# Decay rows read from SBUF, a warming of three matmuls, weight loads behind the rows, and a scheduler that counts transfers at 262 KB per microsecond

## The chip, the cores and the metric

The kernel runs on one core of one Trainium2 chip. The metric is device microseconds of one execution; a lower number is better. The core has five engines with their own queues, each of which works strictly in the order of its program: TensorE (PE, matmuls; its weight loads appear as PEld), VectorE (DVE), ScalarE (ACT), GpSimd (POOL) and SyncE (SP, which here issues the transfers). Engines wait for one another through semaphores. SBUF is the on-chip memory, PSUM holds matmul results in eight banks, HBM is the memory outside.

## The reference

Two parts are computed one behind the other: causal attention with a cumulative decay for 64 heads (8 batches of 8 heads, 576 positions, head size 64), and a feed-forward layer with softplus on the 4608 resulting rows.

```python
scores = scale * np.matmul(q, k.transpose(0, 1, 3, 2))
cum = np.cumsum(np.log(np.clip(f, 0.0001, 1.0)), axis=-1)
decay = cum[:, :, :, None] - cum[:, :, None, :]
scores = np.where(causal, -1000000000.0, scores + decay)
attn = softmax(scores)
x = np.matmul(attn, v)              # then (4608, 512)
h = x @ w_in                        # 512 -> 2048
g = np.maximum(h, 0.0) + np.log1p(np.exp(-np.abs(h)))
out = g @ w_out                     # 2048 -> 512
```

## The kernel before

**Jobs.** Attention is cut into jobs. Jobs 0 to 3 take two heads each of batch 0 and their first 256 positions; jobs 4 to 11 take one head each of batch 0 and its other positions; then follow 56 whole heads of batches 1 to 7. The first twelve are "plain": q, k and two extra rows lie as full fp32 in one of two tiles (T00 and T01, each with two places), and one fp32 matmul per piece makes the scores. The two extra rows hold the cumulative decay of the queries and of the keys and a constant 8 against it, so that the matmul itself adds the decay. Later jobs use tiles T0 and T1, in which q, k and the decay are split into a high and a low part; `raw` is the one buffer into which their q and k are loaded.

**Decay.** `decay` (L358) loads f for all 64 heads, clips it on VectorE (L366), takes the logarithm on ScalarE (L369) and sums along the positions with one scan on VectorE (L374) into the tile `cum`. The sums are stored to HBM (`cum_d`, L377), and the rows of the plain jobs are loaded from there (L639 for a pair of jobs, L644 and L645 for the others). `split` (L382, L383) makes the high and low parts `chl`, which are stored to HBM too (`aug_d`, L387), for the later jobs.

**A job.** `scores` (L747 where plain) fills a PSUM bank of the tag `att`; VectorE takes the row minimum (L754, tile `negm`), ScalarE the exponential (L774), VectorE the inverse sums (L786, L787); the weights are scaled (L796 and L798), turned by matmuls with an identity (L831, tile `b`), copied to SBUF, multiplied with v (L880 where plain, tile `o`), and the result is copied to `x` (`x32`).

**Feed-forward.** Tokens are taken in blocks; block 0 (256 tokens) is plain fp32: `h` (L1024) is the up-projection, in two PSUM banks that take turns; ScalarE makes |h|, exp and log (L1076 to L1082), VectorE adds them to `g` (L1088), and `acc` (L1147) is the down-projection. Later blocks use split numbers (L1043, L1128).

**Weights.** w_in and w_out come as 64-bit floats in 32 tiles of 512 KB, into five staging places (tags `wl` twice, `xh` twice, `xl` once; names `sti`, `sto`, `xh_st`, `xl_st`; L432). Each is converted by a scaling on ScalarE (L436), a clip on VectorE or GpSimd (L439), and three instructions on VectorE (L443, L447, L451; results `woh`, `wol`). A staging place is free again after L447.

**The scheduler.** `Plan.run` walks through all operations at build time, with a cost for each, and writes them to the engines in the order in which it expects them to start; the hardware then follows that order. SP is one of the engines that it plans: a transfer costs SP `on_dma` and lands `dma_lag` later. Where it expects TensorE to idle over 0.5 us before the first down-projection, it writes matmuls without a use there (`fill`, L1320), and `warm` (L1309) writes `WARM` such matmuls at the start. `decay_rest` and the loads of v and of weights are added to the plan at fixed points of `tile_decay_attention_softplus_ffn`.

Of the kernel before, what the change touches and what calls it, by code (L numbers as in the profile page):

```python
# [10 lines left out]
F32 = mybir.dt.float32  # L11
# [3 lines left out]
ALU = mybir.AluOpType  # L15
# [7 lines left out]
COPY_BIAS = 0.1  # L23
WINDOW = 700
PLAIN = 0
WARM = 7
FFN_RANK = 0
# [185 lines left out]
def tile_decay_attention_softplus_ffn(  # L213
# [21 lines left out]
    P = 128  # L235
# [41 lines left out]
    T = {}  # L277
# [22 lines left out]
    aug_d = dpool.tile([BH, 2, S], F32, name="aug_d")  # L300
    cum_d = dpool.tile([BH, S], F32, name="cum_d")

# [52 lines left out]

    decay_ready, cum_used, first_rows = {}, [], []

    def decay():  # L358
        box = {}

        def load(e):
            box["f"] = buf("wl", [P, 1024], "fs")[0:BH, 0:S]
            e.dma_start(out=box["f"], in_=f)

        def clip(e):
            e.tensor_scalar(box["f"], box["f"], 1e-4, 1.0, ALU.max, ALU.min)  # L366

        def log(e):
            e.activation(box["f"], box["f"], AF.Ln)  # L369

        def scan(e):

            box["c"] = buf("x32", [P, NCC, S], "cum")[0:BH, 0, :]
            e.tensor_tensor_scan(box["c"], box["f"], box["f"], 0.0, ALU.add, ALU.min)  # L374

        def store_first(e):
            e.dma_start(out=cum_d, in_=box["c"])  # L377

        def split(e):
            hl = buf("raw", [P, 2, S], "chl", F32R)  # L380
            ch, cl = box["hl"] = hl[0:BH, 0, :], hl[0:BH, 1, :]
            e.tensor_copy(ch, box["c"])  # L382
            e.tensor_sub(cl, box["c"], ch.bitcast(F32))  # L383
# [8 lines left out]
        c = add(On("DVE", 1.36), scan, after=[l], takes=("x32",))  # L392
        give("wl", [c])
        decay_ready["sums"] = add_dma(store_first, BH * S / 256, after=[c])
        cum_used.append(add(NO_ENGINE, mark, after=[decay_ready["sums"]]))
# [180 lines left out]
    def attention(job):  # L576
# [28 lines left out]
        def load_v():  # L605
# [12 lines left out]
            if plain:  # L618
                vtag = st["vtag"] = ("vhl", "vhl", "vraw", "vhl", "vraw")[number % 5]
            st["v"] = add_dma(v, 128 if pair else 160, takes=(vtag,))  # L620
            st["V"] = [st["v"]]

        def load32():
            def qk(e):
# [5 lines left out]
                else:  # L630
                    e.dma_start(out=qk32[0:64], in_=qkT[b, :, heads[0]])

            def rows(e):
                if pair:

                    t0 = T0[number // 2 % 2].rearrange("p t s -> p (t s)")[:, 0:2048]
                    t0 = t0.rearrange("p (i t s) -> p i t s", i=4, t=2)
                    for x in range(2):
                        e.dma_start(  # L639
                            out=t0[64 + x : 65 + x, :, x],  # L640
                            in_=cum_d[bh : bh + 4, 0:256].unsqueeze(0),
                        )
                else:
                    e.dma_start(out=qk32[64:65, 0, qs:qe], in_=cum_d[bh : bh + 1, qs:qe])  # L644
                    e.dma_start(out=qk32[65:66, 1, 0:ke], in_=cum_d[bh : bh + 1, 0:ke])  # L645

# [5 lines left out]
            if not pair:  # L652
                y = add_dma(rows, 4, 2, after=[start, decay_ready["sums"]] + set_)
# [6 lines left out]
            st["T"] = [x, y]  # L660

# [65 lines left out]
        def stat_tile(ti):  # L727
# [42 lines left out]
            for a, z, acc, box in todo:  # L770
# [4 lines left out]

                x = add(on_act(z - a, 0.19, True), weight, after=mins + [st["p"]] + ps_set)
                give("att", [x])
# [517 lines left out]
    for i in range(1, 4):  # L1295
        set_rows0(i)
    ps_set = [fill(x, 0.0, w, [decay_ready["sums"]]) for xs in ps for x, w in zip(xs, PW)]
# [26 lines left out]
    for n in range(len(jobs) + 1):  # L1324
# [87 lines left out]
```

## Time and profile before

| | us |
|---|---|
| median of three runs (1227.13 to 1228.07) | 1227.53 |
| the profiled execution | 1227.12 |
| its span | 1225.1 |
| start of the first scores | 14.30 |
| start of the first up-projection | 67.29 |
| start of the first down-projection | 89.58 |

The profile's page gives the busy time of each engine over the span. A table by windows gives the same for chosen stretches: us of the stretch, then busy us and number of instructions for each engine, the TensorE clock that was granted as a share of full speed (PEclk), the share of time in which the transfer engines were busy, and GB/s. In the timeline each row has its start, its length and, in brackets, how long the engine had idled and for what. In the chain of waits each row has a start, a length and what ended the step before. The groups of one tile give the shortest, median and longest duration in ns. An fp32 matmul stands in the profile as two rows (x16 for 8 matmuls).

### The profile page before, as it was taken

Reading aid. Unit: us, or ns where it says so; the run is one execution under the profiler, and the core shown is the slowest. Engines: PE = TensorE matmul, PEld = TensorE weight load, DVE = VectorE, ACT = ScalarE, POOL = GpSimd, SP = SyncE. Lnnn points to the kernel's source line nnn. Section 1 sums busy time; section 2 is a strip of 40 time slices with the busy share of each in tenths; the row PEclk is TensorE's granted clock in tenths of the full one; section 3 lists DMA queues with packets and bytes.
Section 4 is the critical chain, followed back from the end, with each engine's and each line's share of the span. In section 5 each row is a group of like instructions: output and inputs, shape, how many; then the busy total and the mean of one; then the engine's idle time right before and its main releaser. Section 6 shows DMA issues by size and latency. Waiting matters only on the chain.

```text
span 1225.1 us, 19553 instructions
## 1 busy us (share of the span) xinstructions
PE 1199.9 (98%) x6320; PEld 993.9 (81%) x6320; DVE 869.5 (71%) x2164; ACT 872.9 (71%) x2120; POOL 137.4 (11%) x128
## 2 busy tenths in 40 slices
PE   7899999999999999999999999999999999999998
PEld 5666678888887888888888888888888888888886
DVE  6998889998787678877787778677866774223322
ACT  4676688878787788778886788788867873444543
POOL 3632012010001000110010100110010000000000
PEclk9999999999999999999999999999999999999999
DMA  7874435435446543744464446453565425211210
GB/s 199 254 207 143 137 91 153 111 90 166 128 141 179 166 133 117 228 145 128 137 197 136 141 130 197 139 168 104 153 186 155 138 80 172 69 52 52 86 52 35
DMA packets 100198, 168.38 MB, mean 137 GB/s; under 512 B 10496, under 2 KB 74008, under 8 KB 100096
## 3 DMA queue, kind: packets, MB, share of 16 engines
q1 hardware_dynamic: 100096, 167.13, 46.2%
q8 instruction: 50, 0.82, 0.3%
q14 instruction: 52, 0.43, 0.1%
HBM read 127.85 MB, written 39.24 MB: 136 GB/s over the span
## 4 chain that ended last, share of the span: by engine, by line
PE 84%; DVE 6%; DMA 4%; ACT 4%; issue 1%; SPq 1%; POOL 1%; DVEq 0%; POOLq 0%; ACTq 0%
PE h L1043 29%; PE acc L1128 28%; PE b L831 7%; PE o L886 6%; PE s L750 3%; PE s L749 3%; PE h L1024 2%; PE acc L1147 2%; PE o L880 2%; DMA raw<-in_qkT 2%; PE s L747 1%; ACT p L774 1%; DVE s L754 1%; DMA xh_st<-in_w_in 1%; DVE pl L846 1%
## 5 line engine op out<-in xcount | busy, mean ns | idle before, releaser
L1043 PE MATMUL h<-xh,wih 128*128 128x512 f32 (+1 forms) x576 | 229.5, 401 | 0.7 <-DVE pl L846 0.3
L774 ACT ACTIVATE p<-s,negm 128x288 f32<-128x288 f32 (+7 forms) x384 | 183.0, 479 | 50.3 <-DVE negm L754 46.6
L1043 PE MATMUL h<-xl,wih 128*128 128x512 f32 (+1 forms) x576 | 216.7, 379 | 0.0
L1090 DVE SCALAR_TENSOR_TENSOR h<-h,e 128x512 f32<-128x512 f32 x136 | 95.2, 700 | 136.0 <-ACT e L1082 135.9
L754 DVE CUSTOM_DVE_ANT_0 s<-s,cmask 128x288 f32<-128x288 f32 (+5 forms) x320 | 137.8, 436 | 72.1 <-PE s L750 61.6
L798 POOL TENSOR_SCALAR p<-p,rsum 128x448 f32<-128x448 f32 (+4 forms) x79 | 89.4, 1139 | 784.5 <-PE s L750 192.6
L1076 ACT ACTIVATE e<-h 128x512 f32<-128x512 f32 x144 | 85.7, 595 | 126.4 <-PE h L1043 124.5
L846 DVE TENSOR_TENSOR pl<-b,ph 128x64 fp32r<-128x64 f32 (+1 forms) x224 | 126.3, 569 | 35.0 <-ACT ph L209 33.1
L1043 PE MATMUL h<-xh,wl 128*128 128x512 f32 (+1 forms) x576 | 148.7, 380 | 0.0
L1128 PE MATMUL acc<-woh_dt_float32r,gh 128*128 128x512 f32 x352 | 143.1, 406 | 0.0
L1128 PE MATMUL acc<-woh_dt_float32r,gl 128*128 128x512 f32 x352 | 138.0, 392 | 0.0
L1128 PE MATMUL acc<-wol_dt_float32r,gh 128*128 128x512 f32 x352 | 137.3, 390 | 0.0
L831 PE MATMUL b<-ident,p 128*128 128x128 f32 x784 | 126.5, 274 | 4.8 <-POOL p L798 2.6
L1043 PEld LDWEIGHTS h<-xh,wih 128*128 128x128 f32 x576 | 108.8, 189 | 17.1 <-DVE gl L1098 0.8
L1043 PEld LDWEIGHTS h<-xh,wl 128*128 128x128 f32 x576 | 104.8, 188 | 21.7
L1043 PEld LDWEIGHTS h<-xl,wih 128*128 128x128 f32 x576 | 108.8, 189 | 14.6
L1098 DVE TENSOR_TENSOR gl<-h,gh 128x512 fp32r<-128x512 f32 x136 | 93.4, 687 | 35.1 <-ACT gh L209 34.1
L209 ACT CAST ph<-b 128x512 fp32r<-128x512 f32 (+1 forms) x171 | 85.3, 501 | 41.7 <-PE b L831 40.4
L831 PEld LDWEIGHTS b<-ident,p 128*128 128x128 f32 x784 | 94.4, 140 | 22.6 <-ACT p L796 3.5
L796 ACT ACTIVATE p<-p,rsum 128x192 f32<-128x192 f32 (+6 forms) x219 | 108.6, 556 | 3.4 <-DVE rsum L787 2.8
L749 PE MATMUL s<-T 128*64 128x64 f32 x336 | 98.2, 304 | 2.0 <-ACT p L774 1.3
L886 PE MATMUL o<-ph,vhl 128*128 128x448 f32 (+4 forms) x352 | 98.6, 294 | 0.0
(159 smaller groups left out, 2402.2 us busy)
## 6 DMA issues: line engine op xcount, KB each, us to landing
wl<-wil_d SPq DMA_DIRECT2D x72, 512.0 KB
raw<-in_qkT SPq DMA_DIRECT2D x112, 288.0 KB
g_d<-gh SPq DMA_DIRECT2D x96, 128.0 KB
g_d<-gl SPq DMA_DIRECT2D x96, 128.0 KB
vr<-in_vR SPq DMA_DIRECT2D x64, 160.0 KB
out<-ob SPq DMA_DIRECT2D x36, 256.0 KB
sto<-in_w_out SPq DMA_DIRECT2D x11, 512.0 KB
sti<-in_w_in SPq DMA_DIRECT2D x9, 512.0 KB
```

The lines of the kernel that those rows point to most:

```text
L749: e.matmul(o, qA[:, q0:end], kA[:, a:z], start=True, stop=False)
L754: e.tensor_tensor_reduce(out=box["o"], in0=box["o"], in1=cmask[0:n_q, right - w : right], scale=-0.125, scalar=m0 if i else 3.0e38, op0=AL ...
L774: e.activation(o, box["o"], AF.Exp, bias=m1, scale=-1.0, accum_out=acc)
L796: e.activation(a, a, AF.Copy, scale=f_)
L798: e.tensor_scalar(a, a, f_, None, ALU.mult)
L831: e.transpose(box["ps"][:, at : at + P], pt[pi][:, c : c + P], one)
L846: e.tensor_sub(box["l"], box["ps"][:, 0:w], box["h"].bitcast(F32))
L886: e.matmul(box["ps"][:, a - g0 : z - g0], st["vhl"][:, vc, :], pbox[x][:, o : o + z - a], start=i == 0 and m == 0, stop=i == len(todo) - 1 ...
L1043: e.matmul(o, l, r, start=m == 0, stop=m == 11)
L1090: e.scalar_tensor_tensor(h, h, 0.0, box["e"], ALU.max, ALU.add)
L1098: e.tensor_sub(box["l"], box["t"], box["h"].bitcast(F32))
L1128: e.matmul(st["acc", tt], l, r[fc], start=fc == 0 and m == 0, stop=fc == NFC - 1 and m == 2,)
```

## The change

The rows of the plain jobs are read from the SBUF tile `cum`; `cum_d` and its store are gone. The scan is cut in two (256 and 320 positions), and the rows of jobs 0 to 3 need the first part alone. The second pair's rows are issued from ScalarE's queue. `cum` is held until the last of the rows is read. `decay_rest` (split and store for later jobs) moves from the start to job 2. `WARM` goes from 7 to 3. Weight loads wait in the plan for the first scan instead of the first rows' landing; v of the last plain jobs waits likewise. An exponential waits for the clearing of its own p tile instead of all ten. SP's cost of a transfer is its size at 262 KB per us instead of 360.

```diff
+RATE = 262
-WARM = 7
+WARM = 3
 def on_dma(kb, n=1, eng="SP"):
-    return On(eng, max(0.6 * n, kb / 360 if eng == "SP" else 0.0))
+    return On(eng, max(0.6 * n, kb / RATE) if eng == "SP" else 1.5 * n)
 def dma_lag(kb, n=1, eng="SP"):
-    return 0.6 * (n - 1) + 2.1 + kb / n / 360 - on_dma(kb, n, eng).cost
+    each = 0.6 if eng == "SP" else 1.5
+    return each * (n - 1) + 2.1 + kb / n / RATE - on_dma(kb, n, eng).cost
...
         def scan(e):
-            box["c"] = buf("x32", [P, NCC, S], "cum")[0:BH, 0, :]
-            e.tensor_tensor_scan(box["c"], box["f"], box["f"], 0.0, ALU.add, ALU.min)
-        def store_first(e):
-            e.dma_start(out=cum_d, in_=box["c"])
+            c = cum[0] = buf("x32", [P, NCC, S], "cum")[0:BH, 0, :]
+            x = box["f"][:, 0:256]
+            e.tensor_tensor_scan(c[:, 0:256], x, x, 0.0, ALU.add, ALU.min)
+        def scan_rest(e):
+            c = cum[0]
+            x = box["f"][:, 256:S]
+            e.tensor_tensor_scan(c[:, 256:S], x, x, c[:, 255:256], ALU.add, ALU.min)
...
-        decay_ready["sums"] = add_dma(store_first, BH * S / 256, after=[c])
-        def rest():
-            s = add(On("DVE", 1.05, 0.0, True), split, after=[c], takes=("raw",))
+        def rest(after):
+            s = add(On("DVE", 1.05, 0.0, True), split, after=[c, *after], takes=("raw",))
...
+            later = first_rows if 3 < number < nplain else []
-            st["v"] = add_dma(v, 128 if pair else 160, takes=(vtag,))
+            st["v"] = add_dma(v, 128 if pair else 160, after=later, takes=(vtag,))
...
+            def rows2(e, x):
+                t0 = T0[number // 2 % 2].rearrange("p t s -> p (t s)")[:, 0:2048]
+                t0 = t0.rearrange("p (i t s) -> p i t s", i=4, t=2)
+                e.dma_start(out=t0[64 + x : 65 + x, :, x], in_=cum[0][bh : bh + 4, 0:256])
             def rows(e):
...
+                e.dma_start(out=qk32[64:65, 0, qs:qe], in_=cum[0][bh : bh + 1, qs:qe])
+                e.dma_start(out=qk32[65:66, 1, 0:ke], in_=cum[0][bh : bh + 1, 0:ke])
...
-                need = [start, decay_ready["sums"]] + set_ + T0_set[number % 4 + 1, 1]
-                y = rows_of[number] = add_dma(rows, 8, 2, after=need)
-                first_rows[:] = first_rows or [y]
+                need = [start, decay_ready["first"]] + set_ + T0_set[number % 4 + 1, 1]
+                y = rows_of[number] = [
+                    add_dma(lambda e, r=r: rows2(e, r), 4, eng="ACT" if number else "SP", after=need)
+                    for r in range(2)
+                ]
+                first_rows[:] = [decay_ready["first"]]
+            if not number % 2 or not pair:
+                cum_used.append(add(NO_ENGINE, mark, after=y))
...
-        if n == 1:
-            decay_rest()
+        if n == 2:
+            decay_rest(wrote[0][0][2:])
```

The order that the scheduler writes changes over the first 900 or so of TensorE's 5319 rows; behind them TensorE's rows are the same to the end. Three places, in the words of the order listings (buffer numbers at the ends of names; the first number behind a letter is the job or block):

SP at the start, before, from the load of v for job 4 on (`cum_d` is the copy in HBM, T00 and T01 hold jobs 0 to 3, `sti0` and `sti1` are the first two weight tiles):

```order
L615 DMA vr4_164<-in_vR 128x320
L377 DMA cum_d_105<-cum_162 64x576
L639 DMA T00_72<-cum_d_105 1x4x256 x2
L639 DMA T01_73<-cum_d_105 1x4x256 x2
L432 DMA sti0_186<-in_w_in 128x1024
L387 DMA aug_d_104<-chl_167 64x576 x2
L626 DMA T01_73<-in_qkT 64x4x256
L432 DMA sti1_233<-in_w_in 128x1024
```

SP at the same place in the change:

```order
L641 DMA T00_72<-cum_155 1x4x256 x2
L435 DMA sti0_167<-in_w_in 128x1024
L630 DMA T01_73<-in_qkT 64x4x256
L435 DMA sti1_202<-in_w_in 128x1024
L630 DMA T01_73<-in_qkT 64x4x256
L435 DMA xh_st_237<-in_w_in 128x1024 x2
```

The store of the sums, the rows of T01 and the store to `aug_d` no longer stand ahead of the weight tiles (the rows of T01 are on ScalarE's queue now, the store to `aug_d` stands behind nine weight tiles).

VectorE around the first `g`, which frees the first of the two `h` banks, before (20 tiles are converted ahead of these rows and one, `wol9`, ends with the first of them):

```order
L451 SCALAR_TENSOR_TENSOR wol9_dt_float32_727<-to8_693,wol9_dt_float32_727 128x512
L754 ISA s5_2_0_749,negm1_76<-s5_2_0_749,cmask_74 128x288
L754 ISA negm1_76 128x1
L754 ISA s5_2_288_753,negm1_76<-s5_2_288_753,cmask_74,negm1_76 128x288
L754 ISA negm1_76 128x1
L498 TENSOR_TENSOR wil0_765<-woh0_dt_float32_263,wih_101 128x512
L1088 SCALAR_TENSOR_TENSOR g0_0_771<-h0_0_679,e0_0_742 128x512
```

VectorE around the first `g` in the change:

```order
L804 TENSOR_SCALAR p0_512_94<-p0_512_94,rsum2_89 128x448
L454 SCALAR_TENSOR_TENSOR woh11_dt_float32_777<-ti11_766,woh11_dt_float32_777 128x512
L760 ISA s7_0_0_753,negm3_78<-s7_0_0_753,cmask_74 64x320
L760 ISA negm3_78 64x1
L446 TENSOR_SCALAR wol9_dt_float32_815<-to8_775 128x512
L760 ISA s7_1_0_761,negm3_78<-s7_1_0_761,cmask_74 128x448
L760 ISA negm3_78 128x1
L450 SCALAR_TENSOR_TENSOR wol9_dt_float32_815<-sto8_745,wol9_dt_float32_815 128x512
L1094 SCALAR_TENSOR_TENSOR g0_0_834<-h0_0_575,e0_0_783 128x512
```

`g` stands behind two more jobs' row minima (jobs 6 and 7) than before, and behind 20 whole conversions of weight tiles instead of 21.

TensorE ahead of the third up-projection `h0_2`, the first that needs a freed `h` bank, before:

```order
L831 MATMUL b5_2_842<-ident_66,p1_640_100 128x128
L1024 MATMUL h0_2_815<-x32_0_284,woh4_dt_float32_468 128x256
L1024 MATMUL h0_2_815<-x32_0_284,woh5_dt_float32_470 128x256
L1024 MATMUL h0_2_815<-x32_0_284,woh6_dt_float32_489 128x256
L1024 MATMUL h0_2_815<-x32_0_284,woh7_dt_float32_492 128x256
L747 MATMUL s6_2_0_862<-T01_73 128x288
```

TensorE at that place in the change:

```order
L837 MATMUL b6_1_823<-ident_66,p0_640_95 128x128 x2
L837 MATMUL b6_2_830<-ident_66,p0_384_93 128x128
L837 MATMUL b6_2_830<-ident_66,p0_512_94 128x128
L837 MATMUL b6_2_830<-ident_66,p0_640_95 128x128
L753 MATMUL s7_2_288_838<-T01_73 128x288
L1030 MATMUL h0_2_845<-x32_0_269,woh4_dt_float32_445 128x256
```

One more job is turned (job 6) and one more has its scores (job 7) ahead of `h0_2`; twelve fill matmuls (`fill`) stand ahead of the first of job 6's transposes.

More of the change, by code (lines that the diff above doesn't have):

```diff
@@ L352, in tile_decay_attention_softplus_ffn @@
     halves_set = []
-    decay_ready, cum_used, first_rows = {}, [], []
+    decay_ready, cum_used, first_rows, cum = {}, [], [], {}
     def decay():
@@ L391, in decay @@
         l = add(on_act(S), log, after=[o])
-        c = add(On("DVE", 1.36), scan, after=[l], takes=("x32",))
+        decay_ready["first"] = add(On("DVE", 0.63), scan, after=[l], takes=("x32",))
+        c = decay_ready["sums"] = add(On("DVE", 0.78), scan_rest, after=[decay_ready["first"]])
         give("wl", [c])
-        decay_ready["sums"] = add_dma(store_first, BH * S / 256, after=[c])
-        cum_used.append(add(NO_ENGINE, mark, after=[decay_ready["sums"]]))
-        def rest():
-            s = add(On("DVE", 1.05, 0.0, True), split, after=[c], takes=("raw",))
+        def rest(after):
+            s = add(On("DVE", 1.05, 0.0, True), split, after=[c, *after], takes=("raw",))
             w = add_dma(store, BH * S / 128, 2, after=[s] + first_rows)
@@ L652, in load32 @@
             if not pair:
-                y = add_dma(rows, 4, 2, after=[start, decay_ready["sums"]] + set_)
+                y = [add_dma(rows, 4, 2, after=[start, decay_ready["sums"]] + set_)]
             elif number % 2:
@@ L774, in weight @@
                     e.activation(o, box["o"], AF.Exp, bias=m1, scale=-1.0, accum_out=acc)
-                x = add(on_act(z - a, 0.19, True), weight, after=mins + [st["p"]] + ps_set)
+                x = add(on_act(z - a, 0.19, True), weight, after=mins + [st["p"], ps_set[number % 2, pi]])
                 give("att", [x])
@@ L1296, in tile_decay_attention_softplus_ffn @@
         set_rows0(i)
-    ps_set = [fill(x, 0.0, w, [decay_ready["sums"]]) for xs in ps for x, w in zip(xs, PW)]
+    ps_set = {
+        (j, i): fill(ps[j][i], 0.0, PW[i], [decay_ready["first"]])
+        for i in (3, 4, 2, 0, 1) for j in range(2)
+    }
     for n in range(nfirst):
```

18 lines of the change are left out of this document (3 added, 15 removed).

## The prediction

> **What bounds the kernel now.** I read the page's busy times first, for the whole span, then the windows, to find where TensorE's lost time lies.
>
> ```profile
> PE 1199.9 (98%) x6320; PEld 993.9 (81%) x6320; DVE 869.5 (71%) x2164; ACT 872.9 (71%) x2120; POOL 137.4 (11%) x128
> ```
>
> ```profile
> core 0: us, PE busy (x) PEld busy (x) DVE busy (x) ACT busy (x) POOL busy (x), PEclk, DMA share, GB/s
> 0.00:4.80 4.80, 2.45 (x11) 2.45 (x12) 2.70 (x14) 2.03 (x4) 4.01 (x18) 1.00 0.49 108
> 4.80:14.85 10.05, 10.05 (x47) 6.79 (x46) 4.49 (x9) 0.21 (x2) 1.60 (x4) 1.00 0.58 121
> 14.85:29.50 14.65, 10.82 (x67) 8.12 (x65) 11.71 (x44) 9.78 (x31) 2.61 (x5) 1.00 0.99 287
> 29.50:50.00 20.50, 16.24 (x102) 13.25 (x102) 18.09 (x36) 13.50 (x33) 13.95 (x10) 0.92 0.76 240
> 50.00:67.30 17.30, 15.62 (x101) 12.07 (x102) 17.02 (x42) 11.05 (x27) 10.86 (x5) 1.00 0.91 263
> ```
>
> TensorE is busy for 98% of the span, so anything to be gained is in its idle time and in matmuls without a use. Up to 67.3 us, where the first up-projection starts, it idles 2.35 + 3.83 + 4.26 + 1.68 = 12.1 us, and the fill matmuls hide more:
>
> ```profile
> sum 1225.10, PE 29.59 PEld 27.56; mean PE 5.92 PEld 5.51
> ```
>
> The start is one chain: f, clip, logarithm, scan, the store of the sums, their rows, the first scores. From 14.85 us the transfer engines are full (share 0.99), and from 50 us VectorE is (17.02 of 17.30). VectorE converts the weight tiles and makes the row minima, so **it decides when the first `g` is there** (L1088), and there the change must pay.
>
> **The start.** These are pieces of the chain of waits and of the timeline, the second fence for the weight loads of the warming.
>
> ```profile
> 4.77 1.36 DVE cum L374
> ...
> 6.14 3.66 DMA cum_d<-cum
> ```
>
> ```profile
> 6.56 0.34 PEld L1309 LDWEIGHTS warm<-cmask 128*128 128x128 f32 x1 [0.41 <-issue]
> 7.27 0.19 PEld L1309 LDWEIGHTS warm<-cmask 128*128 128x128 f32 x1 [0.37 <-issue]
> 7.64 0.19 PEld L1309 LDWEIGHTS warm<-cmask 128*128 128x128 f32 x1 [0.19 <-issue]
> ```
>
> ```profile
> 9.86 2.65 SPq L639 DMA_DIRECT2D T<-cum_d  x4
> ...
> 11.40 2.87 PEld L1320 LDWEIGHTS fill<-cmask 128*128 128x128 f32 x25 [0.19 <-issue]
> 12.55 0.44 SPq L432 DMA_DIRECT2D sti<-in_w_in  x1
> ...
> 14.30 3.50 PE L747 MATMUL s<-T 66*128 66x128 f32 x16
> ```
>
> Before, the scores start right behind the fill matmuls; the rows were issued by 12.5 us and did not hold them up visibly. In the change TensorE has 3 warming and 12 fill matmuls ahead of the scores, 6 and 24 halves. Warming halves are 0.71 us apart up to 7.27 us and 0.37 behind; the warming starts at 5.07, so three halves at 0.71 and three at 0.37 end near 8.4, and 24 fill halves at 2.87 / 25 = 0.115 take 2.75: **the first scores at 11.15, 3.1 us sooner.** The rows must be there by then. The first part of the scan is 256 of 576 positions, 1.36 x 256 / 576 = 0.60: done at 5.4. Two issues at 2.65 / 4 = 0.66 end at 6.75. No row shows a transfer from SBUF to SBUF; bounds are 0, and the 3.66 of the 144 KB store to HBM. The larger gives 10.4, still under 11.15, so I take the rows as covered by TensorE's queue; without that cover (shorter filling) they alone would let the scores start near 10. Pair two's issues lie on ScalarE's queue, 2 x 0.66 us that fall in its idle time (0.21 busy of 10.05). `cum` keeps its place longer; its next user in `x32` comes behind the last rows' issue, so I price that at nothing, and at one copy, 0.5 us, if it does wait.
>
> **The weight loads.** They leave SP at 6.75 instead of 12.55, 5.8 us sooner, because the store of the sums, whose landing the rows awaited, and two row issues are no longer ahead of them; `aug_d`, which stood between the first and the second tile, is behind them too. Were the transfer engines free then?
>
> ```profile
> 10.00:13.00 3.00, 3.00 (x20) 2.26 (x19) 0.00 (x0) 0.00 (x0) 0.00 (x0) 1.00 0.02 4
> 32.00:36.00 4.00, 3.00 (x14) 2.03 (x15) 4.00 (x6) 2.34 (x7) 3.91 (x4) 0.81 0.44 103
> 36.00:40.00 4.00, 4.00 (x29) 4.00 (x28) 3.96 (x11) 3.08 (x9) 1.26 (x1) 0.76 0.87 309
> ```
>
> At 10 to 13 us they moved 4 GB/s; the time is free, and what is loaded then is out of the way of the full stretch behind. Counting 262 KB per us is near what the full stretches move (263 and 287). The 240 of the window 29.5 to 50 is lower, so staging places, which come free by conversion, limit too.
>
> **VectorE up to the first `g`.** The third up-projection needs the `h` bank that this `g` frees.
>
> ```profile
> 0.00:77.37 77.37, 65.20 (x371) 50.00 (x372) 63.88 (x166) 45.68 (x115) 35.67 (x41) 0.98 0.79 224
> 67.30:89.65 22.35, 22.30 (x109) 16.16 (x107) 21.05 (x52) 18.78 (x45) 6.61 (x3) 1.00 0.69 192
> 89.65:175.00 85.35, 85.35 (x391) 56.00 (x392) 74.19 (x190) 60.10 (x151) 11.58 (x10) 1.00 0.45 130
> 175.00:280.00 105.00, 101.44 (x665) 88.37 (x664) 97.51 (x257) 85.75 (x227) 14.44 (x12) 1.00 0.42 118
> ```
>
> ```profile
> L451 DVE SCALAR_TENSOR_TENSOR woh_dt_float<-ti,woh_dt_float x16: 660/682/1095, 21.1 to 104.4; 128x512 uint32<-128x512 uint32 x16
> L439 DVE TENSOR_SCALAR ti<-ti x10: 416/424/755, 18.8 to 101.0; 128x512 f32<-128x512 f32 x10
> ```
>
> ```profile
> L754 DVE CUSTOM_DVE_ANT_0 s<-s,cmask x30: 274/432/633, 14.8 to 109.1; 128x128 f32<-128x128 f32 x8, 128x256 f32<-128x256 f32 x8, 64x320 f32<-64x320 f32 x5, 128x448 f32<-128x448 f32 x5
> ```
>
> 77.37 is the end of the first `g`; VectorE was busy 63.88 up to there and idle 13.5. In the new order it does more ahead of it: six more row minima, 288 to 448 wide, between the median 0.43 and the 0.63 of the widest plus a read of about 0.14, some 0.67 each: 4.0; three more clips that GpSimd did, at 0.42: 1.3; two more residual splits of the tile size of L451, at 0.68: 1.4; the rest (more sums, scalings and copies, the scan's second start, against one conversion less and a clearing that went to GpSimd) +0.4 by the nearest rows. Together +7.1: 71.0.
>
> Its idle time was 2.10 + 5.56 = 7.7 up to 14.85, and 5.8 behind. In the change the first 14.85 become 11.75 with 3.1 us less; of the work there, the split for `aug_d` (about 1.3) and one clearing (0.5) have moved behind, so 7.66 - 3.1 + 1.8 = 6.3 idle remain. The later 5.8 is waiting for tiles and clips, which come up to 5.8 us sooner and partly from VectorE itself: between 0 and 5.8 + 3.1 = 8.9 (the start's whole gain lost to later tiles). I take 4, nearer to the first because the loads gain more than the start. The first `g` ends at 71.0 + 6.3 + 4 = **81.3** (77.3 to 86.2). That is later than 77.37, yet TensorE has done more by then.
>
> **What TensorE has done by then.** The next rows give one matmul's price by the distances of starts.
>
> ```profile
> 82.64 1.03 PE L1024 MATMUL h<-x,woh_dt_float 128*128 128x256 f32 x4
> 83.50 0.92 PE L747 MATMUL s<-T 66*128 66x448 f32 x2
> 84.26 0.49 PE L831 MATMUL b<-ident,p 128*128 128x128 f32 x3
> 84.59 1.89 PE L1024 MATMUL h<-x,woh_dt_float 128*128 128x256 f32 x8
> 86.31 1.14 PE L747 MATMUL s<-T 66*128 66x288 f32 x4
> 87.38 2.27 PE L880 MATMUL o<-p,vr 128*64 128x320 f32 x10
> ```
>
> An up-projection matmul takes 0.86 / 2 = 0.43, a transpose 0.33 / 3 = 0.11, scores 0.76 at 448 wide and 1.07 / 2 = 0.535 at 288. Ahead of the new third up-projection stands, against what the old order had ahead of its first down-projection at 89.65: 12 more transposes (+1.3), four more score pieces (0.76, two of 0.535, one of 320 on 64 partitions at about 0.55: +2.4), and eight up-projections fewer (-3.5): +0.2. So at 81.3 it stands where the old one stood at 89.85, **8.5 us ahead** (3.6 to 12.5). TensorE itself can be there: from the first up-projection, which VectorE's share puts near 50 us, it has 20 us of work to the third.
>
> **What is kept.** At that point VectorE is behind: old, 63.88 - 10.07 (the overlap of both windows, 67.30 to 77.37, taken as full) + 21.05 = 74.9 us of work by 89.65; new, 71.0. The 4 us are still owed. VectorE idled 11.2 us from 89.65 to 175 and could pay there, but from 175 to 280 it is 93% busy; from about 280 us the two orders are the same. Kept is between 8.5 - 4.0 = 4.5 and 8.5; I take the middle, 6.5. The profiled execution of 1227.12 becomes 1220.6; the median shown stands 0.4 higher, so **1221.0**.
>
> **The rivals.**
> - *VectorE never waits behind 12 us.* If the earlier loads keep every tile ahead of it, `g` ends at 77.3, the gain is 12.5 and VectorE pays the rest later: 1215. Against: the full transfer engines above.
> - *The loads leave sooner and land no sooner.* If conversion, not issue, gates the staging places, VectorE's idle time stays, `g` is there at 86.2, the gain is 3.6 and the 4.0 of owed work eat it: about 1228, no change. For: the 240 GB/s between 29.5 and 50 with VectorE 18.09 of 20.50 busy.
> - *Slower: the loads into `raw`.* Later jobs load q and k into one buffer, and four such loads lie in the chain of waits between 180 and 300 us, the first and the last of them:
>
> ```profile
> 192.43 4.57 DMA raw<-in_qkT
> ...
> 267.59 4.45 DMA raw<-in_qkT
> ```
>
> The new counting of transfers moves loads of weights against these. One that falls behind a 512 KB load costs 512 / 262 = 2.0 us; five of them exposed make +10 against a gain of 6.5, 1231. It decides from four on. Against: TensorE lost only 3.6 us in that whole stretch, so most waits there are hidden.
> - *The clock.* Ten fewer matmul halves without a use at the start, and other gaps at 32 to 40, where the granted clock was 0.81 and 0.76 behind idle time. If it were at half through those 20 us of work from 50 us, they take 41, end at 91 instead of 81.3, and the gain is gone: 1228. It decides below a clock of about 0.65, and only 0.76 has been seen, with TensorE idle for a whole microsecond of four. The Trainium skill ("TensorE: Matmul & The Clock Gate", "Part 1: The HAM clock gate") says that the array runs at half clock until some 3.4 us of sustained activity and after an idle window of that length; the warming rows above, slow up to 7.27, agree in kind, though TensorE had been busy since about 2.35 (the last 2.45 of the first 4.80 us), 4.9 us earlier. By that rule three warming matmuls with twelve fills behind them, 6 us without a gap, are enough, and only a gap that long would start this rival.
>
> **How the numbers follow.** My forecast, 1221.0 with a range of its own of 1217 to 1225, 0.59; no late waits, 1215, 0.13; no sooner landing, 1228, 0.14; `raw`, 1231, 0.08; the clock, 1228, 0.04; the rest is beyond these. Changes below 0.2%, 2.5 us, cannot be told from none. Faster: the first two cases, 0.72, the edge of the third, 0.02: 0.74. Same: the rest of the third and most of the clock, 0.15. Slower: `raw` and what is left, 0.11. To leave out no more than 0.2 the range runs from 1213 to 1229.5.
>
> **What would show it.** Right: first scores near 11.2; the first weight tile issued near 7; the first `g` ending near 81, VectorE's idle time up to there 10 to 11 us, `h` waiting for VectorE there; the first up-projection near 50. Right in the sum: TensorE's start of a late down-projection is 6 us earlier, the shift being 8 at 90 us and less by 280. Wrong: the first tiles' conversions start no sooner; a `raw` chain that is longer than before; a granted clock under 0.76 before 60 us.

## The result, and the profile after

The changed kernel takes 1210.86 us (median of four runs, 1210.16 to 1213.52) against 1227.33 before: ratio 0.987, 95% interval 0.9853 to 0.9887. The forecast was 1221.0, the range 1213.0 to 1229.5: the side was right, the size 2.5 times too small. The profiled execution has a span of 1209.1 against 1225.1 us.

The page's busy times of the changed kernel, and its table by the windows of before (columns as there):

```profile
PE 1190.6 (98%) x6270; PEld 988.1 (82%) x6270; DVE 859.1 (71%) x2151; ACT 880.2 (73%) x2142; POOL 116.8 (10%) x120
```

```profile
0.00:4.80 4.80, 2.45 (x11) 2.45 (x12) 2.74 (x14) 1.97 (x2) 4.02 (x17) 1.00 0.48 112
4.80:14.85 10.05, 9.27 (x51) 6.79 (x50) 6.43 (x23) 3.88 (x17) 4.13 (x10) 1.00 0.84 214
14.85:29.50 14.65, 13.81 (x91) 10.52 (x91) 14.58 (x39) 13.01 (x35) 7.52 (x6) 1.00 0.87 279
29.50:50.00 20.50, 19.37 (x111) 14.03 (x111) 19.85 (x56) 16.29 (x45) 8.01 (x7) 1.00 0.93 273
50.00:67.30 17.30, 17.30 (x85) 11.77 (x84) 16.16 (x43) 12.59 (x31) 2.22 (x1) 1.00 0.79 224
67.30:89.65 22.35, 20.74 (x97) 14.68 (x96) 19.94 (x48) 15.46 (x35) 2.24 (x1) 0.92 0.50 133
89.65:175.00 85.35, 85.13 (x412) 58.84 (x412) 75.83 (x197) 65.60 (x162) 5.98 (x8) 1.00 0.52 152
175.00:280.00 105.00, 101.89 (x662) 90.05 (x661) 97.22 (x259) 89.77 (x235) 12.57 (x12) 1.00 0.46 133
```

TensorE now idles 2.35 + 0.78 + 0.84 + 1.13 + 0 + 1.61 = 6.7 us up to 89.65, where it idled 12.2. The fill matmuls in the same stretch, of the changed kernel and of before:

```profile
0.00:89.65 89.65, 23.79 (x168) 21.77 (x168) 0.98 0.75 214
```

```profile
0.00:89.65 89.65, 29.59 (x210) 27.56 (x210) 0.98 0.77 219
```

With the warming (2.8 us busy against 6.5) the time that TensorE loses up to 89.65 goes from 12.2 + 29.6 + 6.5 = 48.3 to 6.7 + 23.8 + 2.8 = 33.3. These **15.0 us are nearly all of the gain** of 16.0 in the span. The windows behind 89.65 lose about as much as before (85.13 and 101.89 busy against 85.35 and 101.44).

Where the lead arises shows in the up-projection's group, its first and last start behind the durations, of before and of the change (up to 100 us):

```profile
L1024 PE MATMUL h<-x,woh_dt_float x60: 377/379/483, 67.3 to 99.4; 128*128 128x256 f32 x60
```

```profile
L1030 PE MATMUL h<-x,woh_dt_float x70: 377/379/634, 47.4 to 100.0; 128*128 128x256 f32 x70
```

The first up-projection starts at 47.4 instead of 67.3: TensorE multiplies there where it filled before. The start of everything moved far less. The changed kernel's first weight load and first scores in the timeline:

```profile
7.69 0.35 SPq L435 DMA_DIRECT2D sti<-in_w_in  x1
...
10.36 3.50 PE L753 MATMUL s<-T 66*128 66x128 f32 x16
```

That is 4.9 and 3.9 us sooner than 12.55 and 14.30. So 4 to 5 us at the start became 20 at the first up-projection and 16 at the end, and the experiments ask by what.

### The profile page after: what moved, and what is told of

Its sections match the earlier page's. It is cut to its first block, busy times and chain, and to the rows that moved or that the text cites. A ratio compares the mean times of both kernels' runs of the same rounds, so it can differ in the third digit from the quotient of the medians.

```text
span 1209.1 us, 19425 instructions
## 1 busy us (share of the span) xinstructions
PE 1190.6 (98%) x6270; PEld 988.1 (82%) x6270; DVE 859.1 (71%) x2151; ACT 880.2 (73%) x2142; POOL 116.8 (10%) x120
## 3 DMA queue, kind: packets, MB, share of 16 engines
q1 hardware_dynamic: 100480, 166.98, 47.4%
## 4 chain that ended last, share of the span: by engine, by line
PE 88%; DVE 5%; ACT 4%; DMA 1%; issue 1%; POOL 0%; SPq 0%; DVEq 0%; POOLq 0%; ACTq 0%
PE h L1049 30%; PE acc L1134 29%; PE b L837 8%; PE o L892 7%; PE s L755 3%; PE s L756 3%; PE h L1030 2%; PE acc L1153 2%; PE o L886 2%; PE s L753 1%; ACT p L780 1%; DMA raw<-in_qkT 1%; ACT p L802 1%; DVE s L760 1%; PE fill L1328 1%
## 5 line engine op out<-in xcount | busy, mean ns | idle before, releaser
L780 ACT ACTIVATE p<-s,negm 128x288 f32<-128x288 f32 (+7 forms) x384 | 183.0, 479 | 48.1 <-DVE negm L760 45.1
L804 POOL TENSOR_SCALAR p<-p,rsum 64x64 f32<-64x64 f32 (+2 forms) x78 | 86.4, 1115 | 784.4 <-DVE rsum L793 190.1
L802 ACT ACTIVATE p<-p,rsum 128x192 f32<-128x192 f32 (+6 forms) x224 | 111.4, 557 | 6.4 <-DVE rsum L793 5.7
```

What stands on the lines that cost most here:

```text
L780: e.activation(o, box["o"], AF.Exp, bias=m1, scale=-1.0, accum_out=acc)
L802: e.activation(a, a, AF.Copy, scale=f_)
```

## The experiments

Times are compared by the ratio to the kernel before on the same chip, since the medians of that kernel itself went from 1225.8 to 1227.5 us. In the table, "first h" is the start of the first up-projection, "lost" TensorE's idle, fill and warming time up to 89.65 us, "wait" how long ScalarE stood at a weight tile's scaling for the tile's transfer (up to 75 us), all from the profiles, and "ahead" the number of conversions that stand in VectorE's order ahead of the last row minimum of job 3, the last job that the first up-projection needs; "clock" is the granted clock up to 89.65 us.

| kernel | us | ratio (95%) | first h | lost | wait | ahead | clock |
|---|---|---|---|---|---|---|---|
| before | 1227.33 | 1 | 67.3 | 48.3 | 7.9 | 14 | 0.98 |
| rate_others | 1228.90 | 1.0020 (1.0007 to 1.0034) | 66.1 | 45.3 | 5.3 | 14 | 0.92 |
| half_before | 1227.95 | 1.0009 (0.9999 to 1.0020) | 65.6 | 46.5 | 0 | 14 | 0.94 |
| rate_undone | 1227.34 | 1.0009 (0.9997 to 1.0022) | 69.1 | 48.1 | 5.0 | 15 | 0.92 |
| hold8_before | 1223.45 | 0.9978 (0.9965 to 0.9991) | 64.2 | 43.5 | 7.4 | 6 | 0.94 |
| start_alone | 1222.15 | 0.9971 (0.9959 to 0.9982) | 63.3 | 45.4 | 3.4 | 15 | 1.00 |
| rate220 | 1220.65 | 0.9961 (0.9950 to 0.9973) | 44.7 | 36.1 | 0 | 7 | 1.00 |
| force12_after | 1220.12 | 0.9948 (0.9929 to 0.9967) | 60.2 | 39.0 | 1.2 | 12 | 0.96 |
| rate_alone | 1217.03 | 0.9931 (0.9908 to 0.9954) | 51.4 | 38.7 | 0 | 8 | 0.98 |
| rate_weights | 1216.12 | 0.9909 (0.9891 to 0.9926) | 46.9 | 36.5 | 1.1 | 4 | 1.00 |
| rest_weights | 1214.87 | 0.9907 (0.9882 to 0.9933) | 47.6 | 36.1 | 1.1 | 8 | 0.98 |
| late_loads | 1215.68 | 0.9904 (0.9889 to 0.9920) | 52.6 | 37.3 | 2.5 | 9 | 0.96 |
| half_after | 1214.08 | 0.9899 (0.9883 to 0.9916) | 49.0 | 35.3 | 0 | 9 | 0.98 |
| rows_hbm | 1213.51 | 0.9898 (0.9880 to 0.9916) | 51.7 | 36.2 | 0.5 | 9 | 0.96 |
| rest_300 | 1214.47 | 0.9893 (0.9873 to 0.9913) | 56.6 | 38.9 | 1.8 | 11 | 0.94 |
| rate300 | 1211.82 | 0.9888 (0.9869 to 0.9907) | 55.0 | 40.2 | 2.1 | 11 | 0.98 |
| warm_undone | 1213.43 | 0.9881 (0.9863 to 0.9899) | 48.4 | 34.2 | 0 | 9 | 1.00 |
| hold8_rest | 1211.42 | 0.9875 (0.9852 to 0.9897) | 42.0 | 31.9 | 0 | 5 | 1.00 |
| the change | 1210.86 | 0.9870 (0.9853 to 0.9887) | 47.4 | 33.3 | 0 | 9 | 0.98 |
| rest_undone | 1208.81 | 0.9847 (0.9833 to 0.9862) | 44.8 | 31.4 | 0 | 7 | 1.00 |

The granted clock alone moves the time of one and the same kernel: of the 13 runs of before beside hold8_before, the three with a clock of 0.999 over the whole execution took 1224.2 to 1224.8 us, the three with 0.994 took 1227.3 to 1229.7. "Lost" does not hold this: rate_others and start_alone lost the same (45.3 and 45.4 us), and are 0.5% apart, at a clock of 0.92 and 1.00. So a difference of 0.3% between two kernels can lie in the clock of their runs.

### Start or order

Four kernels split the change: the count alone, all but the count, the start's edits alone, and the change's own order with the rows through HBM again.

```diff
 rate_alone (before)
-    return On(eng, max(0.6 * n, kb / 360 if eng == "SP" else 0.0))
+    return On(eng, max(0.6 * n, kb / 262 if eng == "SP" else 0.0))
 rate_undone (change)
-RATE = 262
+RATE = 360
 start_alone (change)
-RATE = 262
-WARM = 3
+RATE = 360
+WARM = 7
-        if n == 2:
-            decay_rest(wrote[0][0][2:])
+        if n == 1:
+            decay_rest([])
 rows_hbm (change)
+                    e.dma_start(out=cum_d, in_=cum[0][:, 0:256])
-                e.dma_start(out=t0[64 + x : 65 + x, :, x], in_=cum[0][bh : bh + 4, 0:256])
+                e.dma_start(out=t0[64 + x : 65 + x, :, x], in_=cum_d[bh : bh + 4].unsqueeze(0))
```

> The kernel before with one edit: SP's transfers counted at 262 KB per us instead of 360. Theory START (the gain of 16.5 us is the earlier beginning: rows from SBUF, first scores 3.9 us and weight loads 4.9 us sooner, carried through VectorE): the beginning stays as before, so 1224 to 1230. Theory ORDER (the gain is the order that the new count writes): at least half of the gain, 1219 or less.

> The changed kernel with the count put back to 360 KB per us. START: first scores and loads as early as in the change, so most of the gain stays, 1211 to 1215. ORDER: at least half of the gain goes, 1219 or more.

> The kernel before with the start's edits alone (rows from SBUF, scan in two, weight loads waiting for the first scan, a p tile waited for by itself); the count is 360, WARM 7, and the split for the later jobs at its old place. START: 1213 to 1219, less than the whole change since scores come behind seven warming matmuls. ORDER: 1223 or more.

> The changed kernel in its own order, but the first part of the sums is stored to HBM and the rows of jobs 0 to 3 are read from there, as before. First scores near 14 instead of 10.4 us, first weight load near 12 instead of 7.7. START: 3.5 to 5 us slower than the change, 1214.5 to 1216. ORDER: under 2 us slower, below 1213.

ORDER won. The count alone brings 0.7%, and without it nothing of the gain is left (1.0009), though the start stays as early as in the change. start_alone brings 0.3%, less than START and about what ORDER said. In the change's own order the way through HBM costs 0.28%, some 3.4 us, though the two intervals still overlap: less than START asked, more than ORDER allowed; its first weight load was issued at 10.36 and its first scores came at 11.67, sooner than the expectation had them, 2.7 and 1.3 us behind the change. The two parts are not a sum: the edits other than the count are worth nothing at 360 (1.0009) and 0.6% at 262 (0.9931 to 0.987). That start_alone gains 0.3% and rate_undone nothing, with nearly the same edits, goes with their clocks (1.00 and 0.92).

### Which count, and the waits of ScalarE

ScalarE's waits gave a second theory, BLOCK. In the group of scalings (L436) of before, these transfers ended its idle time (us, times):

```profile
  DMA sti<-in_w_in: 4.7, 2
  DMA sto<-in_w_out: 1.5, 1
  DMA xh_st<-in_w_in: 1.1, 2
  DMA xl_st<-in_w_out: 0.6, 1
```

A scaling stands in ScalarE's order where the scheduler thought that its tile had landed; if it had not, everything behind it waited, 7.9 us in sum. In the change and in rate_alone the sum is 0.

```diff
 rate_weights (before)
-        ld = add_dma(load, 512, after=first_rows, takes=(stag,))
+        ld = add(On("SP", 512 / 262), load, after=first_rows, takes=(stag,), lag=2.1)
 rate_others (change)
-        ld = add_dma(load, 512, after=first_rows, takes=(stag,))
+        ld = add(On("SP", 512 / 360), load, after=first_rows, takes=(stag,), lag=2.1)
 late_loads (change; ahead of the first weight load)
+                for i in range(9):
+                    e.dma_start(out=idle_d[i : i + 1], in_=ident[0:1, 0:64])
```

> The changed kernel in its own order, with nine small stores (row 0 of the identity, to HBM) on SP's queue ahead of the first weight load, so that it is issued some 5 us later, near 13 us as before. Theory BLOCK (the count of 262 gains because ScalarE's scalings of weight tiles no longer stand in its queue ahead of their tiles' landing: ScalarE waited 7.9 us for such landings before, 0 in the change): waits of ScalarE for weight tiles come back, 4 us or more in sum, and the time rises by 4 to 8 us, to 1215 to 1219. Rival PLACE (the gain is the earlier place of the up-projections in TensorE's order, whatever ScalarE waits for): under 2 us slower, below 1213.

> The kernel before with the count of 262 KB per us for the 32 weight tiles alone (512 / 262 on SP, landing 2.1 later), 360 for all other transfers. BLOCK: the weights' count is the one that places the scalings, so ScalarE's waits for tiles go to near 0 and the time is that of the count alone, 1215 to 1219. Rival PLACE has no reason to give the weight tiles the whole of it: 1220 to 1227.

> The changed kernel with the 32 weight tiles counted at 360 KB per us again and all other transfers at 262. BLOCK: ScalarE's waits for weight tiles come back, 3 us or more in sum, and most of the gain goes, 1219 to 1227. Rival (any order but that of 360 is better by chance, or the count of all transfers works together): 1209 to 1215.

The weight tiles' count carries the effect: given to them alone it brings 0.9%, taken from them alone it costs the whole gain (1.0020). In late_loads the nine stores put the first load off to 11.01, by 3.3 us only, and cost 0.34% or 4 us, though ScalarE's waits came back as 2.5 us, not 4. With the order kept, then, first weight loads that are 2.7 us (rows_hbm) and 3.3 us (late_loads) later cost 3.4 and 4.2 us, about 1.3 for each; the 4.9 us of the change would be some 6 by that, a rough estimate (each price is good to some 2 us) that fits the 0.6% which the other edits bring at 262.

A sweep of the count was to show whether wait and time go together:

> The changed kernel counted at 300 KB per us. BLOCK: ScalarE's wait for tiles and the time lie between those at 262 (0 us, 1211) and at 360 (5 us or more, 1227), 1212 to 1222, and whichever the wait is, the time goes with it. CHANCE (each order is a draw; the count has no meaning of its own): anything, the wait near 0 with a time over 1220 or the wait over 4 with a time near 1210.

> The changed kernel counted at 220 KB per us, slower than the transfers are. BLOCK: no waits of ScalarE for tiles, and a time near the change, 1209 to 1215, since a tile that is expected late blocks nothing and only starts its conversion later. CHANCE: anything from 1205 to 1227.

At 300 both lie between, the time close to that of 262 (2.1 us, 0.9888). At 220 ScalarE waits for nothing and the kernel is slow: BLOCK missed by 6 us. There TensorE loses 36.1 us up to 89.65, little more than the 33.3 of the change, but more behind, in these windows of rate220:

```profile
89.65:175.00 85.35, 83.46 (x395) 58.35 (x395) 73.83 (x181) 61.54 (x149) 9.66 (x9) 0.96 0.55 162
175.00:280.00 105.00, 100.26 (x639) 86.76 (x639) 94.46 (x258) 90.17 (x231) 17.03 (x16) 0.98 0.44 125
```

1.89 + 4.74 = 6.6 us of idle time stand against 0.22 + 3.11 = 3.3 in the change. The clock is lower there too, 0.96 and 0.98 against 1.00, which is some 5 us more if TensorE's work stretches with it (an estimate: 83.46 x 0.04 + 100.26 x 0.02). That tiles expected late are converted late, and that this is what is paid later, is argued, not shown.

The waits themselves were then taken away without touching the order. Every engine's instructions stay where they were, but each weight load brings only half of its tile, so half of the weights is left out. The other half of a staging place is cleared instead, by 20 instructions more on GpSimd and three on VectorE at the start (the latter are not shown):

```diff
 half_before (before) and half_after (change)
+                nc.gpsimd.memset(s[64:128].bitcast(F32), 0.0)
-            e.dma_start(out=box["s"], in_=src)
+            e.dma_start(out=box["s"][0:64], in_=src[0:64])
```

> The kernel before in its own order of every instruction, but each weight load brings only 64 of the 128 partitions (256 KB; the other half of a staging place is cleared, by GpSimd or at the start by VectorE), so the tiles land sooner. It leaves out half of the weights. BLOCK: ScalarE's waits for tiles go from 7.9 us to under 2, and the time falls by 5 to 10 us, to 1217 to 1222. PLACE (the order itself costs the time): 1224 or more.

> The same half loads in the change's order, where ScalarE never waited for a tile. It leaves out half of the weights. BLOCK: nothing to gain, within 2 us of the change, 1209 to 1213 (GpSimd's clearings may cost the upper end). PLACE: the same. A theory that the transfer engines' speed bounds the first 60 us in either order: 1207 or less.

**BLOCK fell.** In half_before one wait is left in the group of scalings, and that is for GpSimd's clearing:

```profile
  POOL sti L429: 0.9, 1
```

Yet the time is that of before (1.0009), and the first up-projection starts at 65.6:

```profile
L1026 PE MATMUL h<-x,woh_dt_float x60: 377/379/483, 65.6 to 98.6; 128*128 128x256 f32 x60
```

Its windows show what filled the time:

```profile
29.50:50.00 20.50, 17.13 (x95) 14.36 (x96) 18.99 (x32) 10.44 (x24) 13.31 (x10) 0.78 0.54 137
50.00:67.30 17.30, 17.05 (x107) 13.68 (x107) 17.20 (x43) 11.32 (x29) 13.02 (x9) 0.96 0.71 156
```

VectorE is full there (18.99 and 17.20) with no tile late and the transfer engines busy for 0.54 and 0.71 of the time only. Two things may hide a part of what the waits were worth. The clearings cost 0.3%, 3.6 us, in half_after, where no wait was left to remove. The clock was lower (0.78 from 29.5 to 50 us, 0.92 before); but the two runs of half_before with 0.998 and 0.999 over the whole execution, 1225.3 and 1225.4 us, lie with the two of before with 0.999 beside them, 1225.5 and 1225.9. So the waits are worth some 4 us at most, an estimate from these runs, and not the 16. That pointed at what VectorE does first, rather than at what the engines wait for.

### What VectorE does first

VectorE's order says it by the column "ahead". Where the scheduler was left to itself, it has VectorE convert 14 or 15 tiles before job 3's last row minimum at 360, and 4 to 9 at 262. Job 3 is the last of the four whose outputs `x` the first up-projection needs, so the first up-projection comes behind those conversions, w_out's among them, which nothing needs before the first down-projection. Theory PRIORITY: that number sets the first up-projection. Two kernels move it at an unchanged count, by a wait that only the scheduler sees.

```diff
 hold8_before (before) and hold8_rest (change, decay_rest at its old place)
+                if number == 3:
+                    third.append(m)
-        sc = add(on_act(512, 0.04), scale, after=[ld], takes=("fe",))
+        sc = add(on_act(512, 0.04), scale, after=[ld] + third * (at >= 8), takes=("fe",))
-            for _ in range(W_EACH):
+            for _ in range(1 if n < 3 else 9 if n == 3 else W_EACH):
 force12_after (change)
+                first = done_w[:12] if number == 3 else []
-                    On("DVE", 0.2 + (z - a) / 960), row_min, after=[o] + mask_set + stat_set,
+                    On("DVE", 0.2 + (z - a) / 960), row_min, after=[o] + mask_set + stat_set + first,
-        return bt
+        done_w.append(bt)
+        return bt
```

> The changed kernel, counted at 262, with job 3's row minima planned behind the twelfth conversion instead of the ninth (14 instead of 11 ahead of job 4's). PRIORITY: first up-projection at 51 to 60 instead of 47.4, and 1213 to 1220, about 1 to 2 us for each conversion moved ahead. COUNT: 1209 to 1213.

> The kernel before, counted at 360 KB per us, with one rule more for the scheduler alone: the scalings of the weight tiles from the ninth on wait for job 3's row minima (and the later tiles enter the plan behind them). Ahead of the last of these minima VectorE now has 6 conversions instead of 14; ahead of job 4's it has 18 as before. PRIORITY: first up-projection at 45 to 57 us instead of 67, and 1214 to 1221. Rival COUNT (what matters is that all transfers are counted near their true rate, for every engine's order): 1224 or more.

force12_after did as PRIORITY said, at the edge: three more conversions ahead of job 3 move the first up-projection to 60.2 and cost 0.8%, 9 of the 16 us.

```profile
L1032 PE MATMUL h<-x,woh_dt_float x64: 377/379/483, 60.2 to 96.4; 128*128 128x256 f32 x64
```

hold8_before did not: with 6 ahead instead of 14 the first up-projection starts at 64.2 and the gain is 0.2%, against the 5 to 12 us expected. The conversions that were held back all stand between the row minima of job 3 and the last of job 4's then (18 ahead of that one, as before), and TensorE waits there, in the window from 50 and in the list of waits from 45 to 70 us (us in total, times, longest):

```profile
50.00:67.30 17.30, 12.24 (x60) 9.39 (x60) 14.92 (x32) 10.05 (x21) 10.24 (x4) 0.80 0.97 274
```

```profile
PE b L833 <- ACT p L798: 4.3, 1, 4.3
```

So the number ahead of job 3 is not the cause by itself, and neither is the start of the first up-projection: rate220 has it at 44.7 and is slow, rate300 at 55.0 and is good. Shown is that the count of the weight tiles carries the larger part of the gain (rate_weights, rate_others), by orders in which the up-projections start 16 to 20 us sooner (rate_alone, rate_weights), and that taking the waits for tiles out of the old order does not bring it (half_before), although later tiles cost in the change's order (late_loads). CHANCE alone is unlikely: the seven different orders that the scheduler wrote freely with the weight tiles at 262 or 300 gave 0.985 to 0.993, the four at 360 gave 0.997 to 1.002. That it costs to move conversions ahead of attention work on VectorE rests on force12_after alone, whose order differs on the other engines as well, and hold8_before speaks against the simple form of it. Which spacing of conversions and jobs a good order needs is open.

### The small edits, and a better version

```diff
 warm_undone (change)
-WARM = 3
+WARM = 7
 rest_undone (change); rest_weights, rest_300 and hold8_rest have this too
-        if n == 2:
-            decay_rest(wrote[0][0][2:])
+        if n == 1:
+            decay_rest([])
```

> The changed kernel with WARM 7. TensorE's rows are the same but for the first three, so this prices the shorter warming alone: first scores some 1 to 3 us later, 0 to 2 us slower, 1211 to 1213, by BLOCK and by PLACE; 3 us or more by START.

> The changed kernel with the split and the store for later jobs (decay_rest) put back to the start. 1.2 us of VectorE and two issues of SP come back between the first weight loads: 1 to 3 us slower, 1212 to 1214, by both theories; more than 4 us by a theory that the start's queues matter as much as the count.

The longer warming takes the place of nine fill matmuls, leaves every other engine's order as it is and costs 0.1%, well inside the width of the intervals: no effect that these runs can tell. Putting `decay_rest` back to the start was expected to cost 1 to 3 us; it gave the fastest kernel of all, 1208.81, though its interval still touches that of the change. Three tries from there:

> A try for a better version: the changed kernel with decay_rest at its old place and 262 KB per us for the weight tiles alone, 360 for the rest. BLOCK: at least as good as the change, 1205 to 1211, waits of ScalarE for tiles under 1 us. CHANCE: anything from 1205 to 1227.

> A try for a better version: the changed kernel with decay_rest at its old place, counted at 300 KB per us, between the counts that gave 1209 (262, so placed) and 1227 (360). BLOCK: waits of ScalarE for tiles 1 to 3 us, 1208 to 1215; to beat 1208.8 it would have to be under 1207.

> A try for a better version: the change with decay_rest at its old place (1208.8) and the rule of hold8_before, which leaves 5 conversions ahead of job 3's row minima and 6 ahead of job 4's, instead of 7 and 10. PRIORITY without a floor: under 1207. If it is already low enough that something else binds (the later conversions, as at a count of 220): 1208 to 1220.

None came under 1208.8. rest_weights missed its 1205 to 1211, and rest_300 came out at the upper end; both have "first h" near those of faster kernels. Between orders of this quality some 5 us are decided by details that no column of the table holds.

## Why the prediction was wrong

**The start: right.** First scores at 10.36 (forecast 11.15): the warming's weight loads were 0.37 us apart from 5.80 us on in this execution, and from 7.27 on before. First weight load at 7.69 (forecast 6.75). The scores waited for no row, as forecast.

**VectorE up to the first `g`: wrong, the step that failed first.** Forecast were 71.0 us of work, 6.3 idle at the start and 4 later: 81.3. Windows of the change that end with the forecast's 11.75 us, with the first `g` and with the third up-projection's start:

```profile
4.80:11.75 6.95, 6.95 (x41) 5.25 (x39) 3.75 (x11) 0.79 (x5) 2.30 (x7) 1.00 0.77 189
0.00:74.92 74.92, 68.20 (x380) 50.46 (x381) 67.35 (x188) 52.87 (x138) 28.14 (x38) 0.99 0.75 217
0.00:76.08 76.08, 69.36 (x382) 51.34 (x383) 68.51 (x191) 54.02 (x141) 28.14 (x38) 0.99 0.75 215
```

The work was 67.35, the idle time 2.06 + 3.20 = 5.3 up to 11.75 us and 2.3 later: 74.92, below the lower bound of 77.3. The largest error is the work, +3.5 instead of +7.1. The durations of VectorE's instructions up to the first `g` sum to 82.3 us against 76.5, so 5.8 more, but durations of neighbours overlap, and "busy" counts such time once: a sum of durations was set against a busy time. Of the two more residual splits that it counted, one came. And the conversions got shorter, which the forecast held constant. The third instruction of a w_in tile and the first, up to the first `g`, before and after (busy us, mean ns | idle before):

```profile
L451 DVE SCALAR_TENSOR_TENSOR woh_dt_float<-ti,woh_dt_float 128x512 uint32<-128x512 uint32 x12 | 9.1, 779 | 0.0
...
L443 DVE TENSOR_SCALAR woh_dt_float<-ti 128x512 uint32<-128x512 uint32 x12 | 6.1, 533 | 1.3 <-POOL ti L439 1.3
```

```profile
L454 DVE SCALAR_TENSOR_TENSOR woh_dt_float<-ti,woh_dt_float 128x512 uint32<-128x512 uint32 x12 | 8.1, 678 | 0.0
...
L446 DVE TENSOR_SCALAR woh_dt_float<-ti 128x512 uint32<-128x512 uint32 x12 | 5.8, 481 | 0.0
```

GpSimd was busy 35.67 us in that time before and 28.14 after, with fewer clips. The single rows of the timelines up to 75 us show it: of the 21 third instructions before, the seven with no GpSimd instruction beside them took 660 to 693 ns, the 14 beside a clip of GpSimd 678 to 1097, in the mean 826; in the change only six had a clip beside them. The Trainium skill ("SBUF — State Buffer", "SBUF: two separate sides") names a pair of ports that GpSimd and VectorE, in some of its forms, hold in turn for a whole instruction; the rows agree in kind.

**The gate: wrong.** The third up-projection was not held by `g`. TensorE in the change around it:

```profile
72.76 0.44 PE L837 MATMUL b<-ident,p 128*128 128x128 f32 x2 [0.46 <-ACT p L802]
73.78 1.55 PE L837 MATMUL b<-ident,p 128*128 128x128 f32 x7 [0.59 <-ACT p L780]
75.12 1.17 PE L753 MATMUL s<-T 66*128 66x288 f32 x2
76.08 4.30 PE L1030 MATMUL h<-x,woh_dt_float 128*128 128x256 f32 x16
```

`g` was there at 74.92; TensorE came at 76.08, straight from job 6's turns and job 7's scores, and the turns had waited for ScalarE. ScalarE in its turn had stood for VectorE, for the inverse sums of job 6 and not for `g`:

```profile
70.96 0.56 ACT L802 ACTIVATE p<-p,rsum 64x320 f32<-64x320 f32 x1 [2.49 <-DVE rsum L793]
```

So VectorE still set the time here, by another of its results than the forecast had. The forecast also gave TensorE 20 us of work from the first up-projection to the third. It took 76.08 - 47.4 = 28.7 us, 27.06 of them busy, 4.29 with fill matmuls. The count of TensorE's work at that point (+0.2) only translates a start into a lead: 89.85 - 76.08 = 13.8 us, where 8.5 (at most 12.5) was forecast.

**What is kept: wrong.** Of 8.5 the forecast kept 6.5, since VectorE would owe 4 us. At the end nothing had been paid back. The first stores of `out` on SP, before and after:

```profile
190.46 1.34 SPq L1215 DMA_DIRECT2D out<-ob  x2
...
280.42 0.34 SPq L1215 DMA_DIRECT2D out<-ob  x1
```

```profile
178.76 0.82 SPq L1221 DMA_DIRECT2D out<-ob  x2
...
265.71 1.34 SPq L1221 DMA_DIRECT2D out<-ob  x2
```

The lead of 13.8 us is 11.7 at these stores, then 14.7, and 16.0 at the end of the span. VectorE is as busy from 175 to 280 as before (97.22 and 97.51 of 105), and TensorE loses no more there.

**The count of 262: not priced.** The forecast noted that 262 is near what the full stretches move, took the order as it stood, and gave the count no term of its own. The runs gave it the larger part: 0.7 to 0.9% alone, against 0.3% for the start alone, and without it the rest is worth nothing. So the right side came by a path that was priced only in part.

**The rivals.** Nearest was the case in which VectorE never waits behind 12 us (1215), at 0.13. That loads leave sooner and land no sooner (1228) did not come. The rival of the `raw` loads did not come: two are left among the longest pieces of the chain from 170 to 300 us, where four were.

```profile
205.43 4.42 DMA raw<-in_qkT
250.84 4.41 DMA raw<-in_qkT
```

The clock rival did not decide: in the change the granted clock is 0.92 at 67 to 89 us and 1.00 in the other windows. rows_hbm had 0.77 from 14.85 to 29.5 and lost 3.4 us in all.

## What to carry to other kernels

A static order is written from costs, and one cost that is wrong in an early, full stretch moves work on an engine that never shows a wait for it: change such a number alone before anything around it, and vary it both ways (262 and 300 were good, 220 kept 0.4% of the 1.3%). Where the bound is a full engine, ask what it does first: VectorE was busy for 59.8 us of the first 67.3 both in half_before and in the change, and the first up-projection started at 66 in the one and at 47 in the other. A wait that goes with a loss is not yet its cause; half loads in an unchanged order took 8 us of waits away, and the time stayed.

## What the runs showed of the hardware

Rows from one SBUF tile to another landed within 3.3 us: SP's second issue for the rows of jobs 0 and 1 ended at 7.04, and their scores started at 10.36 without a wait for them. VectorE's instructions stretch beside some of GpSimd's. In before, half_before, the change and half_after, up to 75 us, a conversion's third instruction took at most 693 ns with no GpSimd instruction beside it, no more beside one of GpSimd's clearings (13 cases), and up to 1108 beside a clip. The first instruction, which has one input, took at most 428 with none beside it and up to 1916 beside a clearing (half_after). A granted clock of 0.77 from 14.85 to 29.5 us (rows_hbm) went with a loss of 3.4 us in all, its later rows included, while TensorE was idle for 2.1 us of that window.
